# State carries by engine copies and late decays off TensorE, in a chunked state-space scan with a bilinear feed-forward

## Chip, cores and metric

One core of one Trainium2 chip. The metric is the device time of one execution in microseconds (us); the median of the runs counts.

## What is computed

The inputs are x (4 x 8 x 768 x 32), a decay a per step in 0.85 to 0.95, and B and C with 16 state entries per step. For each of the 32 heads (4 batches of 8) the reference runs a linear recurrence by chunks and then a feed-forward on the joined heads (3072 tokens of 256):

```python
for c in range(nc):
    cum = np.cumsum(la, axis=-1)
    L = np.exp(cum[:, :, :, None] - cum[:, :, None, :]) * causal
    M = np.einsum('bhin,bhjn->bhij', Cc, Bc) * L
    y[:, :, sl] = M @ xc + (Cc @ state) * np.exp(cum)[..., None]
    state = decay_full * state + np.sum(Bx, axis=2)
...
h = (x @ w1) * (x @ w2)
return (h @ w3) @ w_out
```

(The loop is shortened; decay_full is the decay over the whole chunk and Bx the outer products of B and x, each decayed to the chunk's end.)

## The kernel before

The kernel cuts the 768 steps into 16 chunks of 48 (`T`), for all 32 heads at once. It multiplies w3 by w_out once (tasks v, e), so that per token two products remain: the gated one, and the output product with `WO`. Each product of 32-bit numbers is three matmuls of a high and a low part (fp32r). The tokens go through the feed-forward in seven slabs (`BL`), 384 or 512 tokens each: slabs 0 to 2 by plain products (tasks l..m), slabs 3 and 4, and 5 and 6, as two pairs by seven products of sums of blocks in place of eight (tasks s0 and s1, with the weight mixes z0 to z3 and the token sums p0 and p1).

There is no scheduler in play: `PLAN` (lines 26 to 95) is a list of some 1,200 tasks, executed in that order, and every engine gets its instructions in the order in which the tasks stand. A word is `task:engine@banks`, with V for VectorE, S for ScalarE and G for GpSimd; a task without an engine is a matmul, or a DMA on SyncE's queue. Each engine's queue is served in order, so an instruction that waits holds all behind it; that goes for SP's DMAs too. The numbers behind @ name PSUM banks (0 to 7), slots of `gs` or slots of `fr`.

The steps of chunk c, as far as they matter here:

- X, N, B: loads of x (into `xe`, two buffers), B (`bn`) and B with C (`bc`).
- The decays. Chunks 8 and 9 load the running sum of log a, broadcast over the rows (K, into `ct`, from the scratch tensor `cd`), subtract the row's own sum (F, line 342) and add the causal mask (G, line 346), in two halves of 128x384. The other chunks (below `DIRECT` = 8 or from `LATE` = 10 on) load small pieces from the scratch tensor `cq` into `ld` and `rd` (K, line 311) and make the same differences by a matmul into PSUM (D, line 319). E is the exponential into `r`.
- W: the state's rows of `r`, on GpSimd. CB: 32 matmuls of 32 rows, C times B, into four banks. M0, M1: the product of CB and the decays on VectorE, into `r`. MX: 64 small matmuls of `xe` and `r` into two banks, which give the chunk's y and, in the first 16 rows, its new state.
- T: VectorE transposes the state's part into `z`. Z0 to Z7 carry eight pieces of 16x128 from `z` to the next chunk's `xe`: up to chunk 8 by copies, from chunk `CARRY` = 9 on by DMAs from SBUF to SBUF. y: the outputs go to `ys`. The next chunk's MX needs all eight pieces.

```python
def carry(e, q, z):
    i = z ^ (q & 1)
    (copy if c < CARRY else lambda e, *t: load(*t))(e, xn[64 * i:64 * i + N, q // 2, 4 * z:4 * z + 4], ZZ[32 * q:32 * q + N, 4 * z:4 * z + 4])
```

The feed-forward's tasks: l(slab).(column block).h and .l split a gated block in `gs` or `g` into the high and low part in a slot of `fr`; d(slab).(block) are the output products (9 or 12 matmuls of 128x256); d.y copies a finished tile of 128x256 into a slot of `gs`, d.x stores it. s(pair).(block).1 to .7 are seven units of three matmuls; p, q, r copy PSUM, y, d, g, k add and multiply on VectorE. q and r write slots of `gs`, so they must wait for the store of what stood there. A mix z(j) makes sums of the weights: B (the sum over 128x1024), s, t, d (differences), H, L (their split into the weights), h, l (the split into `tw`); s(pair).6 and .7 read `tw`.

All helpers are short (lines 148 to 164): mm is line 149, DMAs are line 152, two-operand instructions line 155, copies line 161, activations line 164.

Of the kernel before, what the change touches and what calls it, by code (L numbers as in the profile page):

```python
# [60 lines left out]
d0.7 l1.2.h:S@0 c9.Z7 l1.2.l:V c9.Z3 d1.1 c9.Z1 l1.6.h:S@7 z2.H:V c9.Z4 l1.6.l:V c12.K c11.W1:G d1.2 l2.2.h:S@1 z0.B:V@11,12 c12.N d0.y2:S@3 d1.3
c13.N l1.7.h:S@0 d0.y0:S@13 l1.7.l:V d1.4 c9.y:V d0.y1:S@8 c11.E0:S l2.0.l:V l2.6.h:S@6 c11.CB@2,3,4,5 c11.W0:G c10.MX@0,1 c11.M1:V l2.5.h:S@2
l2.6.l:G c12.D0@4 c10.T:V c10.y:S c12.X c12.D1@5 d1.5 c11.M0:V c10.Z5 c12.E1:S c13.K z0.s:V p0.0.h:S d1.6 c12.W1:G l2.4.h:S@5 c10.Z0 l2.5.l:V c10.Z2
c10.Z1 l2.1.h:S@7 c12.CB@2,3,0,1 l2.2.l:V c14.N d1.7 c12.E0:S c10.Z4 l2.1.l:V c10.Z3 c12.W0:G c10.Z6 c12.M1:V d2.0@4,5 l2.7.h:S@0 c10.Z7 l2.4.l:G
c12.M0:V z0.H:S d1.y0:S@2 l2.7.l:V c13.D0@3 p0.1.h:S c13.D1@2 d2.1 c14.K z0.L:V p0.0.l:V p0.1.l:V c11.MX@0,1 d2.2 c11.y:V c13.E0:S c13.E1:S
p0.2.s:V@7 z0.t:V p0.2.h:S c14.D1@2 s0.0.1@3 c11.T:V p0.6.h:S p0.2.l:G d1.y2:V@4 c11.Z7 d2.3 c11.Z1 c11.Z3 z0.d:V d0.x2 d2.4 c15.N p0.3.s:V@1 z0.h:S
c11.Z0 c11.Z2 p0.5.s:V@0 p0.3.h:S s0.0.5@7 z0.l:V p0.5.h:S s0.1.1@0 d1.y1:S@7 p0.4.s:V@5 d2.5 d1.x1 p0.5.l:V p0.4.h:S d1.x2 c11.Z4 s0.0.q:S@3
z1.B:V@11,12 d2.6 c13.X s0.0.p:S@6 d0.x0 c11.Z6 p0.3.l:V d2.7 c11.Z5 z1.s:G s0.0.6 d2.y0:V@4 d2.y2:S@1 z2.L:G d2.y3:S@0 s0.1.5@1 s0.0.r:V@7
s0.1.p:S@5 z1.t:G s0.0.2 p0.4.l:V z1.H:S s0.1.6 s0.1.q:S@13 z1.L:G d2.y1:V@6 s0.0.7 p0.6.l:V s0.1.r:S@5 z2.d:G s0.1.3 s0.0.d:V s0.1.7 s0.1.y:V
s0.1.2 z1.d:V s0.0.4 s0.1.d:V z1.h:G s0.0.3 z1.l:G s0.2.1@1 s0.0.y:V s0.2.5@4 s0.1.g:V s0.2.p:S@7 s0.1.4 s0.0.g:V s0.2.q:S@11 s0.2.2 s0.1.k:V  # L70
l3.0.h:G@0 s0.2.6 s0.0.k:V c14.D0@0 s0.2.r:S@12 c12.MX@5,6 l4.0.h:V@1 z2.h:S l4.0.l:G s0.2.7 c14.E0:S s0.2.3 s0.2.d:V z2.l:G c12.y:S s0.3.1@0
c12.T:V s0.2.4 s0.2.y:V c12.Z3 s0.3.p:S@3 c12.Z4 s0.3.5@5 d0.x1 l3.1.h:V@2 l3.0.l:G c12.Z6 s0.3.6 s0.3.q:S@3 c14.B d2.x3 s0.4.1@4 s0.3.r:S@9
c13.W1:G c14.X s0.3.3 c12.Z0 c12.Z2 s0.3.7 s0.3.y:V c13.B s0.4.5@6 c15.K s0.3.d:V s0.4.p:S@5 s0.3.2 s0.2.g:V c12.Z7 s0.4.6 d1.x0 s0.3.g:V c12.Z1
s0.3.4 d2.x2 l3.2.h:V@3 l3.3.h:S@7 s0.5.1@3 s0.4.q:V@0 c12.Z5 s0.4.r:S@10 s0.5.5@7 s0.3.k:V s0.4.3 s0.2.k:V s0.5.p:S@0 s0.4.7 c14.E1:S s0.5.q:S@1
s0.5.6 c14.W1:G s0.4.d:V c14.W0:G s0.4.2 s0.5.r:S@2 s0.4.y:V l3.2.l:G s0.5.3 l4.2.h:S@6 s0.4.g:V s0.5.2 c13.W0:G s0.5.y:V l3.4.h:S@5 s0.5.7 l4.2.l:G
s0.5.g:V c14.CB@1,2,6,7 c14.M0:V l3.3.l:G s0.4.4 c14.M1:V s0.6.1@5 s0.5.d:V l3.4.l:G c13.CB@6,7,0,1 c13.M1:V c15.B c15.D1@2 s0.5.4 c13.M0:V l3.1.l:G
s0.6.5@0 s0.5.k:V c15.D0@1 s0.6.q:S@12 c13.MX@6,7 s0.4.k:V s0.6.p:S@3 s0.6.3 c13.T:V c13.y:V c13.Z6 s0.6.6 c15.X c13.Z0 s0.7.1@4 c13.Z1 s0.6.r:S@5
d2.x0 s0.6.2 s0.6.y:V c13.Z5 s0.6.7 c13.Z7 s0.7.p:S@0 c13.Z2 s0.7.5@6 c13.Z3 s0.6.d:V c13.Z4 s0.7.6 d2.x1 s0.7.q:S@11 s0.6.g:V s0.6.4 c15.E0:S
d3.0@3,7 l3.6.h:S@4 s0.6.k:V c15.E1:S s0.7.r:S@4 c15.W1:G c14.MX@1,2 c15.W0:G p1.0.h:S l3.5.h:S@0 s0.7.7 c14.T:V p1.0.l:G c14.Z6 c14.y:S s0.7.3
c14.Z1 s0.7.d:V l3.5.l:G c14.Z5 d3.1 c14.Z4 s0.7.y:V c14.Z7 c14.Z3 l3.6.l:G c14.Z0 c14.Z2 c15.CB@5,6,1,2 c15.M0:V s0.7.2 c15.M1:V s1.0.1@5 p1.1.h:V  # L80
s0.7.4 s0.7.g:V p1.1.l:G c15.MX@1,2 s0.7.k:V l3.7.h:G@2 d3.2 c15.y:S s1.0.p:S@4 p1.2.s:V@2 p1.3.s:V@5 p1.2.h:S s1.0.2 p1.6.h:S p1.3.h:G d3.3
l4.5.h:S@3 p1.3.l:V p1.2.l:V s1.0.6 l4.3.h:G@7 s1.0.5@6 p1.6.l:V s1.1.1@2 p1.4.s:V@2 s1.0.q:S@6 d3.4 p1.5.s:V@10 s1.1.p:S@0 p1.4.h:G s1.0.r:S@5
p1.5.h:V p1.4.l:V s1.1.6 l4.6.h:S@5 p1.5.l:G d3.5 s1.1.r:V@2 s1.0.7 l4.4.h:G@0 s1.1.5@1 l3.7.l:G s1.0.d:V s1.1.7 s1.1.q:S@10 s1.0.4 s1.1.d:V
l4.4.l:G s1.1.3 s1.0.3 s1.1.y:V s1.1.4 s1.0.y:V s1.2.1@1 l4.6.l:V s1.2.5@6 s1.1.2 s1.0.g:V d3.6 s1.2.p:S@4 s1.1.g:V s1.2.q:S@12 s1.1.k:V s1.0.k:V
# [737 lines left out]
```

## Time and profile before

| | us |
|---|---|
| median of three runs (range) | 273.94 (273.57 to 275.25) |
| the profiled execution / its span | 274.92 / 273.1 |
| TensorE matmuls busy, share of the span | 258.8 (95%) |
| VectorE / ScalarE / GpSimd busy | 188.6 (69%) / 128.7 (47%) / 100.3 (37%) |

The execution's time is what the device needs from start to end; the span runs from the first to the last instruction. Busy times overlap, so a share tells what is free, not what bounds. In the rows below PE is TensorE, DVE VectorE, ACT ScalarE, POOL GpSimd, SPq the queue of SyncE. A matmul's length contains its way through the array, so two that follow each other overlap: the price of a piece of TensorE's work is the distance from its start to the next piece's start. Where a row has brackets at its end, they hold the time for which the engine stood idle ahead of it and what ended that.

### The profile page before, as it was taken

The page shows a single profiled execution, that of the slowest core. Times are in us where ns is not written, and L with a number is a line of the kernel's source. Part 1 is how long each engine was busy: PE and PEld are TensorE (multiplying, and loading weights), DVE is VectorE, ACT ScalarE, POOL GpSimd, SP SyncE. Part 2 cuts the span into 40 slices and gives each one's busy share as a digit, 9 for nine tenths or more (in the row PEclk, how much of TensorE's full clock was granted, in tenths as well). Part 3 has the DMA queues.
Part 4 walks back from the last instruction along what each step waited for, and adds up shares of the span by engine and source line. Part 5 has one row for each costly group of instructions (what it writes and reads, how often), then busy time and mean ns, then how long its engine had stood idle before and what let it go on. Part 6 is the DMA issues. An engine that isn't in the chain of part 4 may idle for free.

```text
span 273.1 us, 7416 instructions
## 1 busy us (share of the span) xinstructions
PE 258.8 (95%) x2983; PEld 229.4 (84%) x2984; DVE 188.6 (69%) x348; ACT 128.7 (47%) x271; POOL 100.3 (37%) x131
## 2 busy tenths in 40 slices
...
GB/s 177 363 239 306 241 254 259 271 293 185 275 235 168 245 2 1 92 13 155 102 19 85 64 0 124 103 19 95 29 9 1 0 79 0 4 0 0 4 26 166
DMA packets 25522, 32.12 MB, mean 118 GB/s; under 512 B 8208, under 2 KB 18064, under 8 KB 25488
## 3 DMA queue, kind: packets, MB, share of 16 engines
...
## 4 chain that ended last, share of the span: by engine, by line
PE 68%; DMA 11%; SPq 9%; DVE 4%; issue 3%; ACT 2%; POOL 1%; ACTq 0%; POOLq 0%; DVEq 0%
PE ps L149 68%; SPq L152 9%; DMA xe<-in_x_dram 4%; DMA early<-in_w3t_dram 2%; DMA out_dram<-gs 2%; DMA early<-in_w_dram 1%; DMA xe<-z 1%; DVE fr L155 1%; DMA bn<-in_Bn_dram 1%; POOL fr L155 1%; DVE early L158 1%; DVE early L478 1%; ACT early L164 1%; DVE z L400 0%; ACT gs L161 0%
## 5 line engine op out<-in xcount | busy, mean ns | idle before, releaser
L149 PE MATMUL ps<-wo,fr 128*128 128x256 f32 x576 | 70.7, 280 | 0.0
L149 PEld LDWEIGHTS ps<-wo,fr 128*128 128x128 f32 x576 | 69.5, 189 | 0.8 <-DVE r L155 0.2
L155 DVE TENSOR_TENSOR gs<-gs,ps 128x512 f32<-128x512 f32 (+1 forms) x73 | 43.8, 624 | 25.2 <-PE ps L149 18.8
L149 PE MATMUL ps<-xa,wh 128*128 128x384 f32 (+1 forms) x192 | 54.9, 366 | 0.3 <-DVE xa L155 0.2
L161 ACT COPY gs<-ps 128x512 f32<-128x512 f32 (+2 forms) x49 | 23.4, 496 | 46.4 <-PE ps L149 32.5
L149 PEld LDWEIGHTS ps<-xa,wh 128*128 128x128 f32 x192 | 34.8, 188 | 4.9 <-ACT xa L161 0.4
L155 POOL TENSOR_TENSOR r<-bn,r 128x128 f32<-128x128 f32 x32 | 14.8, 470 | 62.4 <-ACT r L164 23.4
L149 PE MATMUL ps<-op,tw 128*128 128x512 f32 (+1 forms) x144 | 35.6, 365 | 0.0
L149 PE MATMUL ps<-xa,wl 128*128 128x384 f32 (+1 forms) x96 | 34.9, 363 | 0.0
L155 POOL TENSOR_TENSOR fr<-gs,fr 128x512 fp32r<-128x512 f32 (+1 forms) x21 | 25.5, 1229 | 18.7 <-PE ps L149 9.2
L149 PEld LDWEIGHTS ps<-op,tw 128*128 128x128 f32 x144 | 25.7, 188 | 2.7
L149 PE MATMUL ps<-fr 128*128 128x256 f32 x192 | 25.3, 286 | 0.8 <-DVE fr L155 0.8
L149 PEld LDWEIGHTS ps<-fr 128*128 128x128 f32 x192 | 24.0, 191 | 1.8 <-DVE fr L155 1.0
L161 ACT CAST fr<-gs 128x512 fp32r<-128x512 f32 (+1 forms) x24 | 13.9, 587 | 22.9 <-PE ps L149 21.4
L155 DVE TENSOR_TENSOR r<-ps,r 128x384 f32<-128x384 f32 x32 | 17.0, 548 | 8.1 <-PE ps L149 6.6
L149 PE MATMUL ps<-op,wh 128*128 128x512 f32 (+1 forms) x64 | 18.3, 366 | 2.2 <-ACT gs L161 2.2
L149 PEld LDWEIGHTS ps<-xa,wl 128*128 128x128 f32 x96 | 18.0, 188 | 1.9
L149 PE MATMUL ps<-r,xe 64*32 64x64 f32 x1024 | 15.9, 224 | 3.6 <-DMA xe<-z 2.0
L155 DVE TENSOR_TENSOR fr<-gs,fr 128x384 fp32r<-128x384 f32 (+1 forms) x20 | 13.4, 682 | 8.4 <-ACT fr L161 6.1
L149 PEld LDWEIGHTS ps<-r,xe 64*32 64x32 f32 x1024 | 12.1, 105 | 7.8 <-DVE gs L155 1.8
L478 DVE SCALAR_TENSOR_TENSOR early<-early 128x512 uint32<-128x512 uint32 x23 | 17.4, 758 | 1.4 <-ACT early L164 0.8
L164 ACT ACTIVATE r<-ps 128x384 f32<-128x384 f32 x28 | 13.6, 492 | 9.7 <-PE ps L149 9.5
(106 smaller groups left out, 379.1 us busy)
## 6 DMA issues: line engine op xcount, KB each, us to landing
...
```

The source lines that it names most:

```text
L149: pin(nc.tensor.matmul(*args, **kw))
L152: pin((nc.scalar if e == "S" else nc.sync).dma_start(dst, src))
L155: pin((nc.gpsimd if e == "G" else nc.vector).tensor_tensor(*args))
L158: pin(nc.vector.tensor_scalar(*args))
L161: pin(nc.scalar.copy(*args) if e == "S" else (nc.gpsimd if e == "G" else nc.vector).tensor_copy(*args))
L164: pin(nc.scalar.activation(*args, **kw))
L478: pin(nc.vector.scalar_tensor_tensor(m, m, 3, v["wl"].bitcast(U32), ALU.logical_shift_left, ALU.bitwise_or))
```

## The change

`LATE` and `CARRY` are set beyond the last chunk. So chunks 10 to 15 make their decays as chunks 8 and 9 do, by broadcast loads of `cd`, F and G, and all carries are engine copies. A store can name its queue, and the last two (d6.x2, d6.x0) go through ScalarE's. The plan is the same up to v17.M, the last product of the weight precomputation (at about 102 us), and is drawn anew behind it, banks and engines of many tasks included. Of the 707 words behind that place the diff below shows the first line and the last two.

```diff
-LATE = 10
-CARRY = 9
+LATE = 99
+CARRY = 99
...
-v17.M@2,3,-1,-1 c9.X c9.E1:S z2.B:V@9,10 e00.a:S@1 e01.a:S@0 c7.Z6:G c9.G0:V l2.4.m@4,5 c7.Z0:G z3.B:V@11,12 l0.4.h:S@0 c9.E0:S c7.Z4:S c9.W0:G
+v17.M@2,3,-1,-1 c7.Z2:S c9.E1:S c7.Z6:S c7.Z4:S z0.B:V@9,10 e00.a:S@1 c7.Z0:G c9.G0:G e00.b:V@1 l2.7.m@4,5 e10.a:S@2 c10.F0:V c9.W1:G l1.1.h:S@0
...
+l6.6.l:G d6.3 l5.7.l:V l5.6.l:G d6.4 d6.5 d5.6 d5.7 d6.6 d5.y2:V@0 d5.y1:S@1 d5.y0:V@13 d5.x2 d6.7 d5.x1 d5.x0 d6.y2:V@12 d6.y1:S@11 d6.x1
+d6.y0:V@10 d6.x2:S d6.x0:S
...
-                load(out.rearrange("(b s) d -> s b d", b=NB)[t0:t0 + P // NB], v["o"])
+                load(out.rearrange("(b s) d -> s b d", b=NB)[t0:t0 + P // NB], v["o"], e)
```

The code below the plan stands two lines lower after the change (line 149 is line 151). Three places of the new order follow; numbers at the end of a name are those of the buffer.

SyncE's DMAs before, in the stretch where chunks 10 to 12 are carried; `xe<-z` are carries, `ld` and `rd` the pieces for the decay matmuls, `out_0_dram` a store:

```order
L152 DMA xe1_83<-z_91 16x4x32
L152 DMA ld_76<-cq_100 32x2x48
L152 DMA rd_77<-cq_100 2x16x48 x2
L152 DMA xe1_83<-z_91 16x4x32 x3
L152 DMA bn2_86<-in_Bn_dram 128x256
L152 DMA xe1_83<-z_91 16x4x32 x4
L152 DMA ld_76<-cq_100 32x2x48
L152 DMA rd_77<-cq_100 2x16x48 x2
L152 DMA xe0_82<-z_91 16x4x32 x3
L152 DMA out_0_dram<-gs_67 32x4x256
L152 DMA bn0_84<-in_Bn_dram 128x256
L152 DMA xe0_82<-z_91 16x4x32 x2
```

The same part of the new order, from chunk 12's K on:

```order
L154 DMA ct0_80<-cd_99 64x768 x2
L154 DMA xe1_83<-in_x_dram 128x512
L154 DMA bn2_86<-in_Bn_dram 128x256
L154 DMA bn0_84<-in_Bn_dram 128x256
L154 DMA ct1_81<-cd_99 64x768 x2
L154 DMA bc0_87<-in_Ct_dram 128x640
L154 DMA xe0_82<-in_x_dram 128x512
L154 DMA out_0_dram<-gs_67 32x4x256
L154 DMA xe1_83<-in_x_dram 128x512
L154 DMA ct0_80<-cd_99 64x768 x2
L154 DMA out_0_dram<-gs_67 32x4x256
```

The carries are gone from between the loads and stores, and a broadcast load of `ct` in two pieces stands for each chunk's three small ones.

GpSimd before, from the last part of the weight mixes on, with the splits of slabs 3 and 4 (`fr`) and state weights (`r`):

```order
L155 TENSOR_TENSOR gs_67<-gs_67 128x4x128
L161 CAST tw_1655<-gs_67 128x768
L155 TENSOR_TENSOR tw_1655<-gs_67,tw_1655 128x768
L161 CAST fr_73<-gs_67 128x512
L155 TENSOR_TENSOR fr_73<-gs_67,fr_73 128x512
L155 TENSOR_TENSOR tw_1655<-gs_67,tw_1655 128x768
L155 TENSOR_TENSOR fr_73<-gs_67,fr_73 128x512
L155 TENSOR_TENSOR r1_90<-bn1_85,r1_90 128x8x16
L155 TENSOR_TENSOR r0_89<-bn2_86,r0_89 128x8x16 x2
L155 TENSOR_TENSOR fr_73<-gs_67,fr_73 128x512
```

GpSimd in the new order, in the middle of weight mixes 2 and 3 (`gs<-gs`, `gs<-wh,wl`, `tw`); `ct` with `la` is F, `ct` with `mask` is G, `xe<-z` a carry:

```order
L157 TENSOR_TENSOR gs_67<-gs_67 128x4x128
L163 COPY xe1_83<-z_91 16x4x32
L157 TENSOR_TENSOR ct1_81<-ct1_81,la_79 128x384
L157 TENSOR_TENSOR gs_67<-wh_96,wl_97 128x1024
L157 TENSOR_TENSOR ct1_81<-ct1_81,mask_75 128x384 x2
L157 TENSOR_TENSOR tw_1953<-gs_67,tw_1953 128x768
L157 TENSOR_TENSOR gs_67<-gs_67 128x2x256
L157 TENSOR_TENSOR r0_89<-bn2_86,r0_89 128x8x16
L163 COPY xe1_83<-z_91 16x4x32
L163 CAST fr_73<-gs_67 128x512
L157 TENSOR_TENSOR r1_90<-bn1_85,r1_90 128x8x16 x2
L157 TENSOR_TENSOR ct1_81<-ct1_81,la_79 128x384
```

F, G, carries and the sum over 128x1024 of mix 3 now stand among the mixes, ahead of the second half of `tw`.

TensorE before, from chunk 9's CB (`bc`) over chunk 8's MX (`r`, `xe`) to slab 0's first output product (`wo`, `fr`); in brackets the semaphores that an instruction waits for:

```order
L149 MATMUL ps<-bc_88 64x96
L149 MATMUL ps<-bc_88 64x96 [waits DVE_49]
L149 MATMUL ps<-bc_88 64x96
L149 MATMUL ps<-bc_88 64x96 [waits Activation_49]
L149 MATMUL ps<-bc_88 64x96
L149 MATMUL ps<-bc_88 64x96 [waits DVE_49]
L149 MATMUL ps<-bc_88 64x96 x9
L149 MATMUL ps<-r_89,xe_82 32x64 [waits DMAHW3_49,Pool_49]
L149 MATMUL ps<-r_89,xe_82 32x64 x4
L149 MATMUL ps<-r_89,xe_82 32x64 [waits Pool_49]
L149 MATMUL ps<-r_89,xe_82 32x64 x26
L149 MATMUL ps<-wo,fr 128x256 [waits DVE_49]
```

The same place in the new order:

```order
L151 MATMUL ps<-xa,wl 128x512
L151 MATMUL ps<-bc_88 64x96 [waits DMAHW0_49,DVE_49]
L151 MATMUL ps<-bc_88 64x96
L151 MATMUL ps<-bc_88 64x96 [waits DVE_49]
L151 MATMUL ps<-bc_88 64x96 x13
L151 MATMUL ps<-r_89,xe_82 32x64 [waits DMAHW3_49,DVE_49,Activation_49]
L151 MATMUL ps<-r_89,xe_82 32x64 x2
L151 MATMUL ps<-r_89,xe_82 32x64 [waits Activation_49]
L151 MATMUL ps<-r_89,xe_82 32x64 x28
L151 MATMUL ps<-wo,fr 128x256 [waits DVE_49]
```

The MX now waits for VectorE at its start. Its banks are 6 and 7, which the CB ahead of it fills (banks 1, 2, 6, 7; before 1, 2, 4, 5), and which M1 reads.

## Rows read from the trace of the kernel before

**Rows 1.** The page's head.
```profile
span 273.1 us, 7416 instructions
```

**Rows 2.** Busy time by stretch of the span (us); the columns are named in the first row.
```profile
core 0: us, PE busy (x) PEld busy (x) DVE busy (x) ACT busy (x) POOL busy (x), PEclk, DMA share, GB/s
128.00:144.00 16.00, 14.31 (x278) 13.00 (x278) 11.55 (x20) 7.96 (x16) 5.18 (x6) 1.00 0.24 56
144.00:178.00 34.00, 31.84 (x223) 26.77 (x223) 22.77 (x38) 15.12 (x30) 16.40 (x16) 1.00 0.25 75
178.00:202.40 24.40, 22.36 (x375) 17.31 (x373) 13.23 (x23) 6.98 (x14) 10.86 (x11) 1.00 0.17 42
202.40:267.75 65.35, 65.35 (x481) 65.35 (x477) 35.28 (x70) 17.25 (x38) 18.58 (x20) 1.00 0.05 17
```

**Rows 3.** Timeline of TensorE around the late recurrence steps: start, length, what, idle before.
```profile
128.51 0.30 PE L149 MATMUL ps<-r,xe 64*32 64x64 f32 x2
...
131.36 0.59 PE L149 MATMUL ps<-rd,ld 96*128 96x384 f32 x2 [0.87 <-DMA rd<-cq]
131.79 2.22 PE L149 MATMUL ps<-wo,fr 128*128 128x256 f32 x18
...
161.30 0.86 PE L149 MATMUL ps<-r,xe 64*32 64x64 f32 x64
162.09 0.98 PE L149 MATMUL ps<-op,tw 128*128 128x512 f32 x3
...
192.24 0.30 PE L149 MATMUL ps<-r,xe 64*32 64x64 f32 x2
...
194.31 0.96 PE L149 MATMUL ps<-op,tw 128*128 128x512 f32 x3
...
199.21 0.86 PE L149 MATMUL ps<-op,tw 128*128 128x512 f32 x3
...
202.39 0.85 PE L149 MATMUL ps<-wo,fr 128*128 128x256 f32 x5
```

**Rows 4.** TensorE's waits: us in total, times, longest.
```profile
PE ps L149 <- ACT gs L161: 2.2, 1, 2.2
PE ps L149 <- DMA xe<-z: 2.0, 5, 1.1
```

**Rows 5.** The chain that ended last, near 175: start, us, what.
```profile
174.66 2.14 DMA out_dram<-gs
```

**Rows 6.** Timeline of TensorE, six products of 512 columns and the next start.
```profile
189.38 1.52 PE L149 MATMUL ps<-op,tw 128*128 128x512 f32 x6
190.74 1.57 PE L149 MATMUL ps<-wo,fr 128*128 128x256 f32 x12
```

**Rows 7.** Groups of GpSimd instructions by shape: count, busy us, mean ns, idle before.
```profile
L155 POOL TENSOR_TENSOR ct<-ct,mask 128x384 f32<-128x384 f32 x2 | 2.4, 1214 | 1.5 <-DVE ct L155 1.5
L155 POOL TENSOR_TENSOR gs<-gs 128x512 f32<-128x512 f32 x3 | 4.6, 1549 | 5.1 <-DVE gs L155 5.1
L155 POOL TENSOR_TENSOR tw<-gs,tw 128x768 fp32r<-128x768 f32 x2 | 3.7, 1870 | 0.1
L155 POOL TENSOR_TENSOR r<-bn,r 128x128 f32<-128x128 f32 x32 | 14.8, 470 | 62.4 <-ACT r L164 23.4 <-DVE fr L155 14.6 <-DVE gs L155 8.1
```

**Rows 8.** Timeline, a GpSimd and a VectorE instruction near 142.
```profile
142.22 1.31 POOL L155 TENSOR_TENSOR op<-gs,op 128x512 fp32r<-128x512 f32 x1 [5.41 <-ACT op L161]
...
142.41 1.67 DVE L155 TENSOR_TENSOR gs<-gs 128x512 f32<-128x512 f32 x1
```

**Rows 9.** VectorE groups between 144 and 178, the costliest.
```profile
L155 DVE TENSOR_TENSOR gs<-gs,ps 128x512 f32<-128x512 f32 x19 | 12.4, 683 | 7.1 <-PE ps L149 6.6 <-ACT gs L161 0.3
```

**Rows 10.** Timeline of VectorE, the weighting after a CB block.
```profile
111.44 0.56 DVE L155 TENSOR_TENSOR r<-ps,r 128x384 f32<-128x384 f32 x1 [1.03 <-PE ps L149]
```

**Rows 11.** Timeline of the last output copy and the last stores.
```profile
267.75 0.42 DVE L161 COPY gs<-ps 128x256 f32<-128x256 f32 x1 [3.00 <-PE ps L149]
...
268.82 1.83 SPq L152 DMA_DIRECT2D out_dram<-gs  x3
```

More of the change, by code (lines that the diff above doesn't have):

```diff
@@ L61 @@
[L61 to L84, printed above, removed]
@@ L93 @@
-l5.4.l:V d6.7 l5.6.h:G@6 l5.6.l:V l5.5.l:G d5.3 d6.y1:S@0 l5.7.h:V@4 d4.5 d6.y0:V@1 d6.y2:V@4 l5.7.l:V d4.6 d4.7 d5.4 d4.y0:V@5 d4.y2:S@6 d4.y1:S@7
-d4.x2 d4.y3:V@8 d5.5 d4.x3 d4.x1 d5.6 d6.x1 d4.x0 d5.7 d6.x2 d6.x0 d5.y0:V@6 d5.y1:S@8 d5.y2:S@9 d5.x1 d5.x0 d5.x2
+v17.M@2,3,-1,-1 c7.Z2:S c9.E1:S c7.Z6:S c7.Z4:S z0.B:V@9,10 e00.a:S@1 c7.Z0:S c9.G0:G e00.b:V@1 l2.7.m@4,5 e10.a:S@2 c10.F0:V c9.W1:G l1.1.h:S@0
+c8.M1:V c10.F1:G c9.E0:S e10.b:V@2 c7.Z7:S c11.K c10.G1:V l1.0.h:S@1 c9.CB@1,2,6,7 l1.0.l:G l2.7.a:S c9.X c9.M1:V e01.a:S@0 c11.B l1.3.h:G@2
@@ new lines @@
+l2.7.g:V c8.MX@6,7 l0.0.h:S@3 l1.1.l:G l1.2.h:S@4 d1.0@5,4 c8.T:V c10.X l1.4.h:S@5 c10.B c10.G0:V c9.W0:G c8.y:S d1.1 l1.4.l:V e11.a:S@3 l1.2.l:G
+e01.b:V@0 l2.1.m@6,7 l1.5.h:S@1 c8.Z1:V c8.Z5:S c8.Z0:G z0.s:V c8.Z6:S l1.6.h:S@0 c11.F0:G c9.M0:V c8.Z3:S c10.E0:S l1.3.l:V c11.G0:G e11.b:V@3 d1.2
+l2.1.a:S c11.F1:V c10.E1:S d1.3 l0.0.l:G l2.1.g:V c8.Z2:S c12.K c8.Z4:S l1.6.l:V c8.Z7:S d1.4 l1.7.h:S@2 c10.W1:G l1.5.l:V l0.5.h:S@4 c10.W0:G
+c9.MX@6,7 l0.1.h:S@5 l1.7.l:G c10.CB@2,3,0,1 l0.3.h:S@6 c9.T:V c11.X c11.N c11.E0:S c10.M1:V d1.5 c9.Z7:G c9.Z5:G c12.N c9.Z1:S z1.B:V@11,12 c9.Z2:S
@@ new lines @@
+d1.6 l0.2.h:S@1 c9.Z6:G c9.Z0:S l0.1.l:V l2.3.h:S@7 l2.4.m@0,1 c11.G1:V c9.y:S l0.3.l:V l0.4.h:S@0 l0.2.l:V c12.F0:V l0.4.l:V d0.0@6,7 l2.4.a:S
+c12.G0:G c10.M0:V c9.Z4:S d0.1 c9.Z3:S z0.t:V l0.6.h:S@3 l0.5.l:G l2.4.g:V c11.E1:S c10.MX@2,3 z1.s:V l0.7.h:S@5 c13.K c12.F1:G d0.2 c10.T:V z0.H:S
+c10.y:S l0.7.l:V c12.B c11.W1:G d0.3 l2.2.h:S@1 z0.L:V c12.X c11.W0:G c10.Z7:S c12.G1:V c10.Z6:S c11.CB@2,3,0,1 c10.Z1:G c10.Z2:S l0.6.l:V
+l2.5.h:S@6 d1.7 l2.2.l:G c11.M0:V p0.1.h:S c11.M1:V d0.4 c10.Z4:S z0.d:V l2.0.h:S@2 c10.Z3:G d0.5 l2.7.h:S@0 l2.0.l:V c10.Z0:G l2.3.l:V d0.6
@@ new lines @@
+l2.6.h:S@4 l2.5.l:V c10.Z5:S d0.7 l2.1.h:S@3 d1.y0:S@5 l2.1.l:V d2.0@0,1 p0.0.h:S l2.4.h:S@5 p0.0.l:V c12.E0:S z2.B:V@0,1 c11.MX@2,3 d1.y2:S@8
+z0.h:S d2.1 l2.7.l:V d0.y2:S@13 l2.4.l:V d0.y1:S@7 d0.x2 d2.2 c11.y:S z2.s:V c13.X d1.y1:S@4 p0.2.s:G@3 c11.T:V d0.y0:S@2 s0.0.1@7 c12.E1:S l2.6.l:V
+d2.3 c14.K s0.0.p:S@6 c12.W0:G p0.1.l:V c11.Z7:S p0.2.h:S d0.x1 c11.Z1:G c12.CB@2,3,4,5 p0.3.s:V@13 c11.Z4:S c14.B d2.4 c12.W1:G p0.4.s:V@6 d0.x0
+c11.Z6:G p0.2.l:V p0.4.h:S c15.N s0.0.2 d1.x2 z1.H:S z0.l:V d2.5 z2.H:S c13.N z1.L:G p0.6.h:S p0.5.s:V@7 p0.3.h:S d2.6 c14.F0:G c12.M0:V p0.5.h:S
```

41 lines of the change are left out of this document (27 added, 14 removed).

## Prediction

> **What bounds the kernel now.** I read the busy time by stretch first, then TensorE's timeline at the places where that shows idle time, then what TensorE waited for, and only then the other engines. The span is 273.1 us and the profiled execution took 274.92, so 1.82 us lie around the span; that execution is 0.98 above the median of 273.94, from which I subtract what the sum gives [rows 1]. The reader is to see two things in the stretches [rows 2]. From 202.4 to 267.75 TensorE is busy for all of 65.35 us, at a granted clock of 1.00 (the 2.4 GHz level), beside VectorE at 35 and GpSimd at 19 us: there only its own columns count, and the split and product work of the other engines hides completely. From 128 to 202.4 it is idle for 1.69 + 2.16 + 2.04 = 5.89 us. In that stretch stand the recurrence steps of chunks 10 to 15, whose state is carried by DMAs.
>
> TensorE's timeline shows the price of each place, which is more than its idle time since matmuls also start slowly there [rows 3]. A clean MX block (64 small matmuls) takes 162.09 - 161.30 = 0.79 us, and a pair of decay matmuls 131.79 - 131.36 = 0.43. Chunk 10's MX and the pair behind it take 131.79 - 128.51 = 3.28 us, which is 2.06 over 0.79 + 0.43. Chunk 14's MX takes 194.31 - 192.24 = 2.07, or 1.28 too much. From 199.21 to 202.39 stand three products of 512 columns and chunk 15's MX. Six such products take 190.74 - 189.38 = 1.36 us, so three take 0.68 [rows 6], and 3.18 - 0.68 - 0.79 = 1.71 is lost. The list of waits names the carry DMAs for 2.0 us in five pieces, and one wait of 2.2 us for a ScalarE copy into gs [rows 4]. That copy waited for a store of gs that landed at 176.80: it left SP's queue at 174.66, behind carries and decay loads [rows 5].
>
> **The change, part by part.** *Carries.* 48 DMAs (c9.Z0 to c14.Z7) become 26 copies on ScalarE, 19 on GpSimd and three on VectorE, and SP's queue holds none of them between its loads and stores. The three late MX blocks and the pair lose their waits: 2.06 + 1.28 + 1.71 = 5.05 us. Between two late MX blocks the new order leaves TensorE at least 48 output products, or 48 x 2.22 / 18 = 5.9 us [rows 3] (chunk 14 to 15). In that time VectorE has to transpose once and each engine to copy some three times, which I estimate at under 0.42 each, since a copy of more data takes that [rows 11]. So I take the whole 5.05.
>
> *Store wait.* With the carries gone a store stands behind at most a few loads, so I also take the 2.2 us away [rows 4].
>
> *Decays.* Twelve matmuls leave TensorE at 0.43 per pair: 2.6 us [rows 3]. In their place come 24 subtractions and mask additions of 128x384, nine of them placed on VectorE and fifteen on GpSimd (chunk 9's last one moves from VectorE to GpSimd, so GpSimd gains sixteen). VectorE has room: it is busy 22.77 of 34 us from 144 to 178 [rows 2]. GpSimd is the engine to look at, below. The 18 small loads of cq become 12 broadcasts of 192 KB; from 128 on the DMA share is a quarter or less [rows 2], and I cost these at nothing. If that cover were gone, ct would come late and F with it, which is part of the same GpSimd chain.
>
> *Last stores.* Before, the last copy starts at 267.75 and three stores follow one another in SP's queue until 268.82 + 1.83 = 270.65 [rows 11], 0.61 each. After the change SP issues one of them and ScalarE two. The two can begin once the first pair of copies has ended, at about 268.3, and end 1.22 later, at 269.5: 1.15 us saved. No row shows an issue on ScalarE's queue. If it cost nothing, about 2 us would be saved; at twice SP's price, nothing; I take SP's own 0.61, the only row of an issue.
>
> *A new wait.* Chunk 9's CB block now fills banks 1, 2, 6 and 7, and chunk 8's MX, which stands right behind it, writes 6 and 7. So MX has to wait until VectorE has weighted that CB. That instruction takes 0.56 us [rows 10], and with CB's drain and two hand-offs I estimate 0.9 us of idle TensorE; below it 0 (if something earlier holds TensorE anyway), above it 2 (two such instructions and the hand-offs). Behind the MX stand output products of slab 1, which lose nothing more by it.
>
> *GpSimd's stretch.* Between the last output product of slab 2 (d2.7) and the product s0.6.6, which needs the second half of weight mix 3 (z3.l), TensorE has 44 products of three matmuls, 44 x 0.68 = 29.9 us, two MX at 0.79 and two CB of at most as much: some 32.7 us at 0.6 a CB. GpSimd begins its chain (z1.d) about 1.5 us behind d2.7, because VectorE has an output copy (0.42 [rows 11]) and two more instructions to do first, and it loses perhaps 1 us to exponentials that come late; 30.2 us are left. It has to do in that time: nine F and G at 1.21, 10.9; four subtractions of a weight mix at 1.55, 6.2; one sum over 128x1024, taken at twice that, 3.1; two of 768 columns at 1.87, 3.7; seven small ones (state weights and carries) at no more than 0.47, 3.3; three more (a split, its cast and a small difference), estimated at 2.5 in all [rows 7]. That is 29.7 us, so 0.5 us to spare, where before GpSimd was busy 16.40 of the 34 us from 144 to 178 [rows 2]. Cheaper than that: at the 768-column row's 2.43 ns per column F and G cost 0.93, the subtractions 1.25 and the large sum 2.5, the chain 26, and TensorE waits for nothing. Dearer: a VectorE instruction on SBUF beside GpSimd took 1.67 us where one that reads PSUM takes 0.68 on the mean [rows 8, 9], so an instruction held so loses 1.0; if six of GpSimd's lose as much, z3.l is 5.5 us late. I take 1.5 us, nearer to the row means, which leave it just in time, than to the upper end, since most of VectorE's work in that stretch reads PSUM.
>
> A rule of the Trainium skill speaks against the change here. SBUF — State Buffer, section "Who interferes with whom", says that a VectorE instruction with two SBUF inputs contends with a GpSimd instruction that reads SBUF, and that whichever comes second is held until the first has ended. The 1.67 us agree, and so do the PSUM-reading instructions at 0.68, which the rule spares. By the rule alone each F or G on GpSimd may hold a split or be held by one, and the sum would go to the second rival's time.
>
> **Sum.** Gone: 5.05 + 2.2 + 2.6 + 1.15 = 11.0. Added: 0.9 + 1.5 = 2.4. That is 8.6 us less: the span 264.5, with 1.82 around it 266.3 for an execution like the profiled one, and 273.94 - 8.6 = 265.3 against the median.
>
> **Rivals.** First, the store wait stays. SP's queue is still served in order, and stores of slabs 0 to 2 still stand behind loads that wait for an MX; but the slots that they free are used again several us later. Then 265.3 + 2.2 = 267.5. Second, GpSimd becomes the bound in part: its instructions grow by 20%, 29.7 x 0.2 - 0.5 = 5.4 us of wait in place of 1.5, or 269.2. For it speaks the missing room, against it that few of VectorE's instructions there read SBUF twice. Third, the other side: the same stretch decides all. Without any GpSimd wait the change would give 263.8; the gain of 10.1 us is spent when GpSimd's chain grows by (10.1 + 0.5) / 29.7 = 36%, with F and G at 1.65 in place of 1.21. At 45% the wait is 12.9 and the time 276.7, slower than before. Before, its instructions kept their means beside a VectorE busy for two thirds of the time, which speaks against that much.
>
> **How the numbers follow.** I give 0.6 to the forecast (262 to 267), 0.12 to the store wait, 0.18 to GpSimd in part, 0.06 to the third, and the rest to waits that I have not seen. The lower end is the sum without both added waits, 273.94 - 11.0 = 262.9, and about 1 us more for slow starts of matmuls that I did not price: 261.8. The upper end, 270.5, takes in the second rival and the dear end of the new wait. About 1% is what a measurement can tell here, so faster means below 271.2: 0.6 + 0.12 + 0.16 with a little of the rest is 0.87; same gets 0.07 from the dear end of the second rival and unseen waits; slower 0.06.
>
> **What would show it.** In the changed profile TensorE should reach c15.MX with no wait for a DMA, should stand idle for some 0.9 us at about 106, should have no wait for gs near 175, and should end near 259 to 260. F and G on GpSimd near 1.2 us and an idle TensorE of at most 2 us between 170 and 182 bear out the GpSimd term; F and G above 1.5 there, with TensorE waiting for tw or GpSimd, would make the prediction wrong, and so would a wait for a carry's copy of more than 1 us in front of a late MX.

## The result, and the profile after

The changed kernel takes 263.49 us (median of four, 262.72 to 264.28), the kernel before beside it 273.75: a ratio of 0.9622, 95% interval 0.9579 to 0.9666. Measured again, as e9_after, it was 264.44 and 0.9675 (0.9624 to 0.9726). Forecast were 265.3 us and a range of 261.8 to 270.5. (In the diff ahead of the prediction one engine letter is wrong: in the new line that begins with v17.M, c7.Z0 goes to ScalarE, S. Of e12_tail there is no undisturbed profile, so only its times are read.)

The head of the page of after (the profiled execution took 263.44 us; TensorE is busy for 97% of the span):

```profile
span 261.6 us, 7416 instructions
```

The busy time by stretch of after, columns as in [rows 2]:

```profile
102.40:128.00 25.60, 24.83 (x433) 22.20 (x431) 22.53 (x36) 19.28 (x48) 18.47 (x24) 1.00 0.44 132
128.00:144.00 16.00, 16.00 (x218) 15.27 (x217) 15.39 (x23) 12.16 (x27) 7.17 (x9) 1.00 0.39 120
144.00:178.00 34.00, 34.00 (x276) 27.45 (x275) 25.41 (x43) 20.19 (x42) 26.27 (x27) 1.00 0.22 68
178.00:202.40 24.40, 24.40 (x364) 21.93 (x363) 18.37 (x32) 11.37 (x27) 14.96 (x21) 1.00 0.05 13
202.40:257.00 54.60, 54.60 (x396) 54.60 (x395) 29.55 (x57) 12.01 (x27) 18.85 (x21) 1.00 0.06 20
```

TensorE is busy all the time from 128 us on, where it was idle for 5.89 us before [rows 2]. What is left stands in TensorE's timeline of after:

```profile
101.28 0.63 PE L151 MATMUL ps<-xa,wh 128*128 128x512 f32 x2
...
105.48 0.85 PE L151 MATMUL ps<-r,xe 64*32 64x64 f32 x64 [0.77 <-ACT fr L163]
...
167.28 0.84 PE L151 MATMUL ps<-op,tw 128*128 128x512 f32 x3
...
178.32 0.86 PE L151 MATMUL ps<-r,xe 64*32 64x64 f32 x64
179.10 0.98 PE L151 MATMUL ps<-op,tw 128*128 128x512 f32 x3
...
251.78 5.70 PE L151 MATMUL ps<-wo,fr 128*128 128x256 f32 x47
```

The 0.77 us ahead of chunk 8's MX is the forecast new wait (the view names a ScalarE split; by the order the MX needs VectorE's M1 at its start, which ran from 104.82 to 105.38). It is the only wait of the eight MX blocks behind 102 us, and all eight last 0.85 or 0.86 us. A clean one takes 179.10 - 178.32 = 0.78 us to the next start (chunk 13's), where chunk 14's took 2.07 before [rows 3].

**A ruler for all runs.** The two profiled executions differ by 274.92 - 263.44 = 11.5 us, over 10 by the medians, and part of that is no effect of the change: the product behind v17.M, up to which both plans are the same, starts at 102.40 us before and at 101.28 after. So traces are compared below from that start to the end of TensorE's last product. TensorE's timeline of before:

```profile
102.40 0.63 PE L149 MATMUL ps<-xa,wh 128*128 128x512 f32 x2
...
244.94 23.13 PE L149 MATMUL ps<-wo,fr 128*128 128x256 f32 x195
```

Before, that is 268.07 - 102.40 = 165.67 us; after, 257.48 - 101.28 = 156.20, so 9.47 less. From there to the end of the span it is 5.03 before and 4.12 after. The forecast had 5.05 + 2.2 + 2.6 - 0.9 - 1.5 = 7.45 for the first piece and 1.15 for the second.

| kernel | ratio to before, 95% interval | ruler, us | TensorE idle in it | its end to the span's end |
|---|---|---|---|---|
| before | 1 | 165.67 | 6.03 | 5.03 |
| after | 0.9622 (0.9579 to 0.9666) | 156.20 | 0.77 | 4.12 |
| e9_after (after again) | 0.9675 (0.9624 to 0.9726) | 156.27 | 0.77 | 4.12 |
| e1_carry | 0.9777 (0.9727 to 0.9827) | 158.11 | 0.04 | 5.04 |
| e2_decay | 1.0421 (1.0333 to 1.0508) | 179.03 | 12.71 | 4.96 |
| e3_both | 1.0062 (1.0027 to 1.0098) | 165.92 | 6.92 | 4.98 |
| e4_dma_carry | 0.9728 (0.9682 to 0.9774) | 158.59 | 2.42 | 4.18 |
| e5_sp_stores | 0.9681 (0.9631 to 0.9730) | 156.26 | 0.77 | 4.47 |
| e10_sp_stores (e5 again) | 0.9665 (0.9619 to 0.9711) | 156.27 | 0.77 | 4.48 |
| e6_banks | 0.9647 (0.9608 to 0.9685) | 156.03 | 0.53 | 4.21 |
| e7_pad | 0.9698 (0.9645 to 0.9752) | 158.36 | 2.44 | 4.12 |
| e8_products | 0.9759 (0.9707 to 0.9810) | 158.61 | 0.77 | 4.21 |
| e11_ahead | 1.0029 (0.9988 to 1.0071) | 164.41 | 4.83 | 4.95 |
| e12_tail | 0.9987 (0.9945 to 1.0028) | | | |

An interval is 1.0 to 1.4 us wide to each side for most, the ruler repeats within 0.1 us (after twice, e5 and e10), so terms of a microsecond are read from the ruler and the verdicts from the ratios. Of before and of each kernel with many waits there is one trace, so how well the ruler repeats there is not known.

### The profile page after: what moved, and what is told of

The parts are those of the page before. It is cut to its first block, busy times and chain, and to the rows that moved or that the text cites. A ratio compares the mean times of both kernels' runs of the same rounds, so it can differ in the third digit from the quotient of the medians.

```text
span 261.6 us, 7416 instructions
## 1 busy us (share of the span) xinstructions
PE 254.0 (97%) x2972; PEld 226.2 (86%) x2972; DVE 196.8 (75%) x354; ACT 141.4 (54%) x308; POOL 121.3 (46%) x160
## 4 chain that ended last, share of the span: by engine, by line
PE 85%; DMA 5%; DVE 4%; ACT 3%; issue 1%; SPq 0%; DVEq 0%
PE ps L151 85%; DMA xe<-in_x_dram 2%; DMA bc<-in_c_dram 2%; ACT fr L163 1%; DVE gs L157 1%; DMA gs<-in_Bt_dram 1%; DVE early L480 1%; DVE fr L157 0%; DVE early L160 0%; SPq L154 0%; ACT g L163 0%; ACT r L166 0%; DVE z L402 0%; ACT early L166 0%; ACT wo L163 0%
## 5 line engine op out<-in xcount | busy, mean ns | idle before, releaser
L157 DVE TENSOR_TENSOR gs<-gs,ps 128x512 f32<-128x512 f32 (+1 forms) x73 | 43.6, 623 | 15.9 <-PE ps L151 10.4
L163 ACT COPY gs<-ps 128x512 f32<-128x512 f32 (+2 forms) x53 | 25.3, 492 | 47.6 <-PE ps L151 41.9
L157 POOL TENSOR_TENSOR r<-bn,r 128x128 f32<-128x128 f32 x32 | 16.0, 507 | 35.5 <-ACT xe L163 13.6
L151 PE MATMUL ps<-fr 128*128 128x256 f32 x192 | 25.4, 286 | 0.2 <-DVE fr L157 0.2
L163 POOL COPY xe<-z 16x128 f32<-16x128 f32 x40 | 15.8, 394 | 14.4 <-issue 5.1
L163 ACT COPY xe<-z 16x128 f32<-16x128 f32 x65 | 19.2, 296 | 1.6 <-DMA xe<-in_x_dram 0.3
L163 POOL CAST fr<-gs 128x384 fp32r<-128x384 f32 (+1 forms) x10 | 6.0, 601 | 28.5 <-PE ps L151 20.1
L166 ACT ACTIVATE early<-early 128x512 f32<-128x512 f32 x23 | 15.5, 675 | 6.1 <-DMA early<-in_w3t_dram 2.8
```

Source lines behind the costliest of these rows:

```text
L151: pin(nc.tensor.matmul(*args, **kw))
L157: pin((nc.gpsimd if e == "G" else nc.vector).tensor_tensor(*args))
L163: pin(nc.scalar.copy(*args) if e == "S" else (nc.gpsimd if e == "G" else nc.vector).tensor_copy(*args))
L166: pin(nc.scalar.activation(*args, **kw))
```

## The experiments

### The parts in the old order: e1_carry, e2_decay, e3_both

The kernel before with the carries as engine copies and nothing else (48 words of the plan get an engine):

```diff
-CARRY = 9
+CARRY = 99
...
-c10.Z5 c10.Z0 c10.Z2
+c10.Z5:G c10.Z0:S c10.Z2:S
```

> The kernel before with its own order; only the 48 carries of chunks 9 to 14 become copies (per chunk four on ScalarE, three on GpSimd, one on VectorE, at the places of the DMAs). If the parts of the change add up, the three late MX waits (5.05 us) and the store wait (2.2) go: 266.5 to 269 us, with TensorE waiting for no carry and no gs near 175. If the gain lies in the order drawn anew, less than 2 us come of it: 272 to 274.

Measured: 266.95 us beside 272.83. The busy time by stretch of e1_carry shows TensorE without a gap:

```profile
101.85:128.00 26.15, 26.15 (x389) 23.51 (x389) 21.99 (x37) 18.30 (x43) 16.97 (x23) 1.00 0.25 77
128.00:178.00 50.00, 49.97 (x553) 42.85 (x547) 40.31 (x66) 26.97 (x59) 29.80 (x34) 1.00 0.19 58
```

The ruler falls by 165.67 - 158.11 = 7.56 us, where the forecast's carries and store wait come to 7.25. By the runs it is 5.9, with 4.7 to 7.4 inside the interval. The wait for gs went with the carries, as the forecast said.

The kernel before with the decays on VectorE (F) and GpSimd (G), carries still DMAs, each F and G where its D stood (12 words like this one):

```diff
-LATE = 10
+LATE = 99
...
-c10.D0@3
+c10.F0:V c10.G0:G
```

> The kernel before with its own order and its DMA carries; only the decays of chunks 10 to 15 change, each decay matmul replaced at its place by a subtraction on VectorE and a mask addition on GpSimd. If the parts add up: 2.6 us of TensorE and the wait of 0.9 for the small loads go, 270 to 271.5 us. If the gain lies in the order drawn anew, the differences come too late at the old places and nothing is gained: 273 to 275.

And both edits in the old order:

> The kernel before in its own order with both edits (carries and decays), stores as before. If the parts add up: about 9.5 us less, 263.5 to 266 us, so that the new order itself is worth at most 1 to 2 us beyond the stores. If the order is what counts: 268 us or more.

Measured: 285.05 us for the decays alone, slower by 4.2%, and 274.49 for both, slower by 0.6%. On top of e1 the decay edit costs 165.92 - 158.11 = 7.8 us of the ruler (7.5 by the medians). Alone it costs 179.03 - 165.67 = 13.4 of the ruler but 12.2 by the medians: the profiled execution of e2, 286.85 us, was 1.8 above the median. TensorE's timeline of e2_decay and then that of e3_both show where:

```profile
117.60 1.60 PE L149 MATMUL ps<-wo,fr 128*128 128x256 f32 x7 [2.26 <-POOL fr L155]
...
186.26 1.22 PE L149 MATMUL ps<-op,wh 128*128 128x512 f32 x2 [3.06 <-ACT gs L161]
```

```profile
117.99 1.08 PE L149 MATMUL ps<-wo,fr 128*128 128x256 f32 x7 [2.26 <-POOL fr L155]
...
145.05 0.50 PE L149 MATMUL ps<-xa,wh 128*128 128x512 f32 x1 [1.98 <-DVE xa L155]
```

In both, a split on GpSimd comes 2.26 us late for an output product. GpSimd's timeline of e3_both shows what held it up:

```profile
112.68 1.26 POOL L155 TENSOR_TENSOR ct<-ct,mask 128x384 f32<-128x384 f32 x1 [1.67 <-DVE ct L155]
114.44 1.39 POOL L155 TENSOR_TENSOR ct<-ct,mask 128x384 f32<-128x384 f32 x1 [0.50 <-DVE ct L155]
...
116.63 2.28 POOL L155 TENSOR_TENSOR fr<-g,fr 128x384 fp32r<-128x384 f32 x2
```

Each G waits for VectorE's F, and the split (`fr<-g,fr`) is queued behind both. The granted clock falls behind this idle place of TensorE, as the stretches of e2_decay show:

```profile
116.00:118.00 2.00, 0.40 (x3) 0.40 (x4) 1.94 (x5) 1.93 (x6) 2.00 (x3) 0.98 0.01 3
118.00:121.00 3.00, 3.00 (x102) 2.50 (x101) 1.68 (x3) 1.01 (x2) 2.16 (x3) 0.50 0.02 5
121.00:122.00 1.00, 1.00 (x20) 0.88 (x7) 1.00 (x3) 0.00 (x0) 0.17 (x1) 0.83 0.00 0
```

From 118 to about 121.7 the clock is at 0.50, the lower level of 1.2 GHz, though TensorE is busy. The sum for e2 by the ruler: 12.71 - 6.03 = 6.7 us more idle time, some 8.2 us of clock (0.06, 0.07, 0.06 and 0.02 missing in stretches of 26.9, 50, 27 and 75.1 us), less 2.6 for the products: 12.3 of the 13.4 of the ruler.

### Is it the place? e11_ahead

e3_both with VectorE's two subtractions of chunk 10 moved ahead:

```diff
-e10.b:V@2 c7.Z2:G
+e10.b:V@2 c10.F0:V c10.F1:V c7.Z2:G
...
-c10.F0:V c10.G0:G l0.3.l:V c10.F1:V c10.G1:G
+c10.G0:G l0.3.l:V c10.G1:G
```

> Both edits in the order of before (274.5 us when run, a ratio of 1.006), with one move: VectorE's two subtractions for the decays of chunk 10 (F0 and F1) stand some 25 entries earlier, ahead of the place where GpSimd waits for them (1.67 and 0.50 us, with its splits queued behind the two mask additions). Theory (the decay edit loses in the old order because in-order GpSimd stands still at the old place, so that its next split is 2.3 us late for TensorE at 118 us, and because the granted clock falls to 0.5 for some 3.6 us behind that idle stretch, which costs half of it, 1.8 us more): GpSimd's two waits go, TensorE's idle stretch at 118 us falls to under 0.4 us, the granted clock stays at 1.00 there, and the time falls by 3 to 4.5 us, to a ratio near 0.992. Rival 1 (VectorE is full there, and the two subtractions only push the lateness on): an idle stretch of over 1.5 us stays within 12 us of the place, less than 1.5 us gained. Rival 2 (the idle stretch goes but the clock falls whatever TensorE does there, as the draw of the chip): 1.8 to 2.6 us gained, granted clock under 0.9 in 118 to 124 us.

TensorE's timeline, and then the busy time by stretch, of e11_ahead:

```profile
115.72 1.07 PE L149 MATMUL ps<-wo,fr 128*128 128x256 f32 x7 [0.43 <-POOL fr L155]
...
143.10 0.50 PE L149 MATMUL ps<-xa,wh 128*128 128x512 f32 x1 [2.00 <-DVE xa L155]
```

```profile
118.00:122.00 4.00, 3.49 (x35) 3.18 (x27) 4.00 (x8) 1.59 (x4) 3.04 (x3) 1.00 0.82 242
...
145.00:150.00 5.00, 5.00 (x27) 4.67 (x26) 4.96 (x9) 2.37 (x5) 3.94 (x5) 0.69 0.00 2
```

The first half of the theory holds: the place was the cause, and the idle time of 2.26 is 0.43 with the clock at 1.00 behind it. The second half falls: the clock falls at another place instead, behind the 2.00 us at 143, where e3 had 1.98 us and kept 1.00. Whether it falls there is not fixed by the place. The ruler gains 165.92 - 164.41 = 1.5 us, and the ratios (1.0029 against 1.0062) overlap. One place is cured, and TensorE is still idle for 4.83 us of the ruler, at others.

### Undoing parts in the new order: e4_dma_carry, e8_products

After, with the carries of chunks 9 to 14 as DMAs again (`CARRY = 9`):

> The changed kernel with its new order and its decays, but the carries of chunks 9 to 14 as DMAs again on SyncE's queue. If the carries cost what the waits of the kernel before showed (5 to 7.3 us): 268.5 to 271 us, with TensorE waiting for xe from a DMA in front of the late MX blocks. If the new order hides a carry whichever way it goes (5 us or more of other work between two MX blocks): within 1.5 us of 263.5.

Measured: 265.77 us; the ruler is 158.59 - 156.20 = 2.39 us longer. TensorE's timeline of e4_dma_carry:

```profile
123.17 0.27 PE L151 MATMUL ps<-r,xe 64*32 64x64 f32 x2 [0.30 <-DMA xe<-z]
124.33 0.84 PE L151 MATMUL ps<-r,xe 64*32 64x64 f32 x62 [0.89 <-DMA xe<-z]
...
179.76 0.86 PE L151 MATMUL ps<-r,xe 64*32 64x64 f32 x64
...
187.61 0.92 PE L151 MATMUL ps<-r,xe 64*32 64x64 f32 x64
...
195.28 1.30 PE L151 MATMUL ps<-r,xe 64*32 64x64 f32 x64 [0.36 <-DMA xe<-z]
```

Neither end of the expectation came: the DMAs cost a third of what they cost before, and nothing waits for gs. Where they cost less, SyncE's queue is what differs in the traces, as at chunk 14 (no run isolates it). Between the MX blocks of chunks 13 and 14 TensorE has 7.0 us of other work in both (from 184.38 + 0.86 to 192.24 before, from 179.76 + 0.86 to 187.61 in e4), and yet chunk 14's MX is torn before (2.07 to the next start, [rows 3]) and whole in e4. TensorE's timeline of before at chunk 13's MX, then SyncE's queue of before behind it, and then that of e4_dma_carry:

```profile
184.38 0.86 PE L149 MATMUL ps<-r,xe 64*32 64x64 f32 x64
```

```profile
185.78 0.58 SPq L152 DMA_DIRECT2D xe<-z  x1
186.54 0.70 SPq L152 DMA_DIRECT2D xe<-in_x_dram  x1
...
188.55 0.60 SPq L152 DMA_DIRECT2D out_dram<-gs  x1
189.19 3.15 SPq L152 DMA_DIRECT2D xe<-z  x5
```

```profile
181.16 5.35 SPq L154 DMA_DIRECT2D xe<-z  x8
```

Before, a load and a store stand among the eight carries, and the last is issued 192.34 - 185.24 = 7.1 us behind the MX; in e4 nothing stands among them, and it is 186.51 - 180.62 = 5.9. The steps themselves are not all further apart: taking e1 for the old order, chunk 11's MX has 9.4 us of other work ahead of it for 7.8 and chunk 15's 6.3 for 5.6, but chunk 10's only 7.6 for 9.2, and there e4 loses most, 0.30 + 0.89. The copies and the new order both pay for the same idle time; their gains don't add.

After, with twelve products of the size of the decays' given back to TensorE (decays still on VectorE and GpSimd; the products' result is not used):

```diff
+            if c >= 10:
+                for hf in range(2):
+                    mm(psum[b[0]][:, :HG * T], LD[:KD].rearrange("p h m -> p (h m)"),
+                       RD[:KD, hf * HG:(hf + 1) * HG].rearrange("p g s -> p (g s)"), start=True, stop=True)
             for n in range(2):
```

> The kernel after, with the twelve TensorE products of 96 rows and 384 columns given back that the late decays took before (two per chunk from chunk 10 on, in front of the chunk's C-B products and into a bank that these then fill; their result is not used, the decays themselves stay on VectorE and GpSimd). Theory (TensorE has no slack from 128 us on, so each product costs its full 0.22 us): 2.4 to 2.9 us slower than the kernel after, near 266.1 us. Rival (the new order has gaps in TensorE's work that take some of them): under 1.2 us slower, under 264.7 us.

Measured: 266.12 us; the ruler is 2.41 us longer. In TensorE's timeline of e8_products a pair takes 175.49 - 175.04 = 0.45:

```profile
175.04 0.52 PE L151 MATMUL ps<-rd,ld 96*128 96x384 f32 x2
175.49 0.59 PE L151 MATMUL ps<-bc 32*64 32x96 f32 x32
```

So the decays' products cost TensorE about what the forecast took (2.6), in an order that leaves no gap.

### What GpSimd has to spare: e7_pad

```diff
-z3.B:G@12,13
+pad.0:G pad.1:G pad.2:G pad.3:G pad.4:G pad.5:G pad.6:G pad.7:G z3.B:G@12,13
...
+    PAD = sb([P, 256], F32, "pad")
+    for i in range(8):
+        task(f"pad.{i}")(lambda e, b: tt(e, PAD, lf, lf, ALU.add))
```

> The kernel after, with eight further GpSimd additions of 128x256 (no result of theirs is used), some 0.65 to 0.77 us each, 5.2 to 6.2 us together, in front of the first split of the last weight slab (z3.B). Theory (GpSimd's chain from z1.d to z3.l has 2.4 us to spare before TensorE needs its end): TensorE waits 2.8 to 3.8 us for GpSimd's split near 179 us, and the time is 3 to 4 us over the kernel after, near 267 us. Rival 1 (the spare is much larger than the order of the rows tells, since later products can stand in): no wait for GpSimd, within 0.5 us. Rival 2 (an idle TensorE also costs granted clock, as in the runs with both edits in the old order, where it fell to 0.72 for 4 us behind an idle stretch of 2.3): the wait as in the theory and a granted clock under 0.9 in the 5 us behind it, 4.5 to 6 us over the kernel after, near 268.5 us.

GpSimd's timeline of e7_pad, and then TensorE's:

```profile
157.71 5.45 POOL L157 TENSOR_TENSOR pad<-la 128x256 f32<-128x256 f32 x8
...
167.42 1.84 POOL L157 TENSOR_TENSOR tw<-gs,tw 128x768 fp32r<-128x768 f32 x1
```

```profile
169.49 0.96 PE L151 MATMUL ps<-op,tw 128*128 128x512 f32 x3 [1.67 <-ACT ps L163]
```

The wait is 1.67 us, less than the theory's 2.8 to 3.8, and at another place: not at the end of the chain but at the second half of `tw` of mix 2, which ends at 167.42 + 1.84 = 169.26 (the view names ScalarE, which had long been done). The end of the chain came 3.9 us later than in after (180.59 for 176.73), and with TensorE itself later by then no product waited for it. The ruler is 2.16 longer; the clock stayed at 1.00.

### TensorE's last wait, and the stores: e6_banks, e5, e10, e12

After, with the wait ahead of chunk 8's MX taken away by other banks:

```diff
-c9.CB@1,2,6,7
+c9.CB@0,1,6,7
...
-c8.MX@6,7
+c8.MX@2,3
...
-e10.a:S@2 c10.F0:V
+e10.a:S@2 e01.a:S@0 e11.a:S@3 c10.F0:V
-e10.b:V@2 c11.K
+e10.b:V@2 e01.b:V@0 e11.b:V@3 c11.K
```

(c7.Z7 moves ahead too.)

> The kernel after, with the one wait of TensorE that is left behind 82 us taken away: chunk 8's mixing product writes banks 2 and 3, chunk 9's C-B products banks 0, 1, 6 and 7, so that the mixing product no longer waits for VectorE to read the bank that the C-B products of chunk 9 filled; the evictions of the two lower slabs stand earlier, to free the banks in time. Theory (TensorE is the bound, each of its idle stretches counts in full): the 0.77 us in front of chunk 8's mixing product goes, 0.6 to 0.9 us faster than the kernel after, about 262.7 us where that has 263.5. Rival (VectorE and ScalarE are as late as before and TensorE meets them at the next product): the idle stretch moves to another place within 10 us, and the time is within 0.3 us of the kernel after or up to 1 us slower.

TensorE's timeline of e6_banks:

```profile
104.92 0.86 PE L151 MATMUL ps<-r,xe 64*32 64x64 f32 x64
106.30 2.39 PE L151 MATMUL ps<-wo,fr 128*128 128x256 f32 x18 [0.53 <-DVE gs L157]
```

The rival was right: 0.77 becomes 0.53 half a microsecond later, 0.2 us in the ruler, nothing in the time. No run beat after.

The last two stores on SyncE's queue again (`d6.x2 d6.x0` without `:S`), run twice, the second time beside after:

> The kernel after, with one thing undone: the last two stores (d6.x2 and d6.x0) are issued by SyncE again instead of ScalarE. Theory (the last stores queued behind each other on SyncE, at about 0.6 us an issue, and that is what the shorter tail saves): 0.6 to 1.2 us slower than the kernel after, so about 264.4 us where that has 263.5, and the stretch from TensorE's last product to the end of the span goes from 4.1 back to about 5.0 us. Rival (the tail is set by how long a store takes to land, whoever issues it): within 0.3 us of the kernel after, the stretch stays at 4.1 to 4.4.

> The kernel after with its last two stores issued by SyncE again, a second time, beside the kernel after on the same chip. Theory, as the trace of the first such run had it (from TensorE's end to the end of the span 4.47 us, where the kernel after has 4.12): 0.2 to 0.5 us slower than the kernel after. Rival (the 1.15 us of the prediction was right, and the medians of the first run, some 1.3 to 1.6 us above, tell the same): 0.9 to 1.6 us slower.

> The kernel before, with the last two of its three stores (d5.x0 and d5.x2) issued by ScalarE's queue and nothing else changed. Theory (each SyncE issue of 0.6 us at the end counts, so two of the three come off the path, and ScalarE issues them one behind the other as its last copies end): 0.3 to 0.7 us faster than the kernel before, TensorE's end to the end of the span 4.3 to 4.7 us where before has 5.04. Rival 1 (all of the 1.15 us of the prediction is the stores' queue): 0.9 to 1.2 us faster. Rival 2 (a store by ScalarE takes longer to land or to issue than by SyncE): within 0.2 us or slower.

The last stores in the timelines of after (ScalarE's queue) and then of e5_sp_stores:

```profile
257.97 1.30 ACTq L154 DMA_DIRECT2D out_dram<-gs  x2
```

```profile
256.60 3.76 SPq L154 DMA_DIRECT2D out_dram<-gs  x6
```

The queue is worth 4.47 - 4.12 = 0.35 us, in both traces. The last issue ends 257.97 + 1.30 - 257.48 = 1.79 us behind TensorE's last product with ScalarE and 256.60 + 3.76 - 258.23 = 2.13 with SyncE. The times can't tell it from nothing: the median of e5 was 264.80, above after's 263.49, but e10 beside after had 263.58 for 264.44 (0.9665 with SyncE, 0.9675 with ScalarE). e12, the kernel before with its last stores by ScalarE, is inconclusive (0.9987, 0.9945 to 1.0028).

## Why the prediction was right, and where its terms were off

- **Carries 5.05, store wait 2.2**: 7.56 in the old order (e1) for 7.25. Right, but not a price of DMA carries as such: in the new order they cost 2.39 (e4).
- **Decays 2.6**: 2.41 (e8). Right as TensorE's share. Not forecast was that this edit loses 7.8 us where F and G stand in the old places, or 12 to 13 without the carries' copies. The prediction took the new order for granted and counted the edits one by one; by e3 and after, order and stores together are worth a ratio of 1.0062 down to 0.9622. As a list of what leaves TensorE the sum holds: 7.56 + 2.41 + 0.91 - 0.77 = 10.1 of the 9.47 + 0.91 = 10.4 measured. As prices of the edits it doesn't, since 7.56 is from the old order and 2.41 from the new. In the new order the parts undone are worth 2.39, 2.41 and 0.35; if these add, about half of the 10.4 comes with the order. No run has the new order without both edits, so that share is not shown.
- **New wait 0.9**: 0.77, at 105.48.
- **GpSimd's stretch 1.5**: no wait at all. This is the mis-sized term, and most of why 263.49 came and not 265.3 (by the ruler 9.47 for 7.45). Two steps of it were off. The durations came from few instructions of before [rows 7]. The groups of GpSimd of after, answering to them, and then its timeline:

```profile
L157 POOL TENSOR_TENSOR ct<-ct,mask 128x384 f32<-128x384 f32 x9 | 11.3, 1264 | 4.4 <-issue 2.4 <-DVE ct L157 1.9
...
L157 POOL TENSOR_TENSOR ct<-ct,la 128x384 f32<-128x384 f32 x9 | 8.3, 926 | 0.1
...
L157 POOL TENSOR_TENSOR gs<-gs 128x512 f32<-128x512 f32 x4 | 5.2, 1308 | 2.7 <-DVE gs L157 2.7
...
L157 POOL TENSOR_TENSOR gs<-wh,wl 128x1024 f32<-128x1024 f32 x1 | 2.4, 2407 | 0.0
```

```profile
146.66 1.34 POOL L157 TENSOR_TENSOR gs<-gs 128x512 f32<-128x512 f32 x1 [2.74 <-DVE gs L157]
...
154.23 0.41 POOL L157 TENSOR_TENSOR r<-bn,r 128x128 f32<-128x128 f32 x1 [2.52 <-ACT r L166]
...
161.64 1.87 POOL L157 TENSOR_TENSOR tw<-gs,tw 128x768 fp32r<-128x768 f32 x1
...
167.66 0.61 POOL L163 CAST fr<-gs 128x512 fp32r<-128x512 f32 x1 [2.17 <-DVE gs L157]
...
174.86 1.87 POOL L157 TENSOR_TENSOR tw<-gs,tw 128x768 fp32r<-128x768 f32 x1
```

F takes 0.93 on the mean where G takes 1.26, and the prediction took a mean of two G's for both; in the chain the five F took 0.81 to 0.83 each and three of the four G 1.00 or 1.01. The mixes' subtractions took 1.31 for 1.55, the large sum 2.41 for 3.1. The chain runs from 146.66 to 176.73, 30.1 us, of which 2.52 + 2.17 = 4.7 are waits for other engines: 25.4 of work where 29.7 were taken, at the cheap end (given as 26, though its terms add up to 25.4; likewise 0.6 + 0.12 + 0.16 is 0.88 without any of the rest). And TensorE came later than 30.2: it asked for the end of the chain at 179.10, so 32.4 us stood against the chain. The prediction also looked at one due place. An earlier one is mix 2's `tw`, done at 163.51 and asked for at 167.28, so 3.77 us early; e7's 5.45 us of additions ahead of it made TensorE wait there for 1.67, which is the difference.
- **Second and third rival, and the rule of the Trainium skill.** VectorE instructions with two SBUF inputs did get longer beside GpSimd. The timeline of VectorE of after:

```profile
147.24 1.31 DVE L157 TENSOR_TENSOR op<-ys,op 128x512 fp32r<-128x512 f32 x1
```

It began while a GpSimd subtraction ran (146.66 to 148.00, above); the two of the same shape, `op<-gs,op`, took 0.73 on the mean between 144 and 178, and the 23 that read PSUM kept their 683 ns [rows 9]. GpSimd's own were held too: the G that began at 147.96, while that VectorE instruction ran, took 1.46 for 1.00, and over the whole trace F took from 0.82 to 1.28. But in the chain this one of nine is the only one that is much longer than the others. The rule of the Trainium skill, SBUF — State Buffer, section "Who interferes with whom", agrees with the 1.31, the 1.46 and the 683, as it did with [rows 8, 9]; that F or G would be held so often as to make GpSimd the bound, no trace here shows.
- **Tail 1.15**: 0.91, of which 0.35 is the queue; the other 0.56 goes with the new order of the last evictions, by the difference and not by a run of its own. An issue by ScalarE took 0.65 where 0.61 was taken for it; oversized was what the queue costs: the forecast had the last issue end 269.5 - 268.07 = 1.4 us behind TensorE's end with ScalarE and 2.6 with SyncE, and in the new order it was 1.79 and 2.13.
